# A lead-in whose last three tiles are mixed by way of HBM, and new lists that order it

## The chip, the cores and the metric

The kernel runs on one core of a Trainium2 chip. Its time is the device time of one launch in microseconds, the median of several runs. TensorE (PE) multiplies, VectorE (DVE) and ScalarE (ACT) work element by element, GpSimd (POOL) does little here, SyncE (SP) issues the DMA transfers, in the order of its program.

## What is computed

```python
# q, k, v: (8, 8, 576, 64); chunks of 64 rows, no work across chunks
scores = scale * q_c @ k_c^T                     # per chunk
attn   = exp(scores - max) / (sum + 1e-9)
x      = (attn @ v_c)  ->  (8, 576, 512)
# low-rank mix over the 576 rows of a batch, rank 32
u   = x + (x^T @ U @ V)^T
out = u + relu(u @ w_ch1) @ w_ch2                # 512 -> 2048 -> 512
```

All products of the mix and of the two layers are made from a high and a low part of each number (fp32r), three products for one.

## The kernel before

Eight batches are taken in four pairs of 2 × 576 rows, nine tiles of 128 rows each; a name such as u_6 or x_7 is a tile of the pair, and (1,2) is tile 2 of pair 1. Three tiles are a group. The weights are 16 chunks W0 to W15, each 512 KB, brought in raw and split into high and low parts (DVE lines 109 to 116 and 385). A block (g, f) takes group g through chunk f: twelve products of 384 columns make h (L815), ACT and DVE make hh and hl of it (L824, L829), and three sets of three products of 512 columns add to o (L842). Names are h_g_f; sc_1_0 are the scores (L541) and av_1_0 the weighted sums (L589) of tile 0 of pair 1.

The lead-in is everything up to the first block of group 2 of pair 0: the attention of the nine tiles of pair 0, the projection by U (y, ys), the mix (u, L748, then x + u on DVE, L754), the splitting of the weights and the 32 blocks of groups 0 and 1. A planner (order(), L161) writes its instructions out by hand. It takes the order of blocks on PE from STRETCHES, the order of SyncE's loads from LOADS (T5: q and k of tile 5; v5: its v, four transfers on L471; U, V, W0), and the rank of the other steps from WORK. HOLD delays two loads of v. The loads of v named in SOFT are issued from GpSimd's queue. After as many blocks as GATES names, the attention of tiles (1,0) and (1,1) may begin. From block HALVES_FROM on, one transfer a block copies a half of the heads of q or k of the next pair, rearranged, from HBM to HBM (halfq, halfk, L421, 2304 pieces of 128 B); the loads qn and kn (L453) of a tile of that pair read these copies, and DVE transposes them (qT, kT, L497).

For pairs 1 to 3, x + u goes out to HBM by four DMAs (us_td, L488, 2048 pieces of 128 B), comes back as one tile (us, L432), and is transposed by DVE (uT, L497). The exponentials of a tile go the same way (es_td, L493; es, L432; eT). In pair 0, u is transposed by four PE products for each tile (ut, L760). Then ACT casts (uth, L782) and DVE subtracts (utl, L787). For tiles 6 to 8 this happens after the last block of group 0.

After the lead-in a hand-written list sets the order of the main loop; its last string is LAST, for the last pair: one word for each o group of three products, u4 being the mix of tile 4, p4 the projection of tile 4, a dot nothing.

Of the kernel before, what the change touches and what calls it, by code (L numbers as in the profile page):

```python
# [23 lines left out]
def kernel(  # L24
# [23 lines left out]
    NF = DF // P  # L48
# [1 line left out]
    GT = 3  # L50
    NEARLY = 9
    PLAIN = 2
    SOFT = (2, 4)
    NX = 9
    SLOTS = {"qk": 3, "e": 1, "eT": 1, "vn": 2, "us": 1, "uT": 1}
    XROOM = 3
# [34 lines left out]
    w1 = {}  # L91
    w2 = {}
# [33 lines left out]
    rank = [0]  # L126
# [611 lines left out]
    def mix_ops(pr, t, x, ys, after=None, first=None):  # L738
        n = f"{pr}_{t}"
        st = {}  # L740
        g, j = divmod(t, GT)
# [49 lines left out]
        ad = Op("DVE", 0.69, add, lr, free="bank")  # L791
        if (pr, t) == (0, 0):
            Op("PE", 0.01, end_filling, lr, free="bank")
        if pr > 0:
            pu = Op("SP", 2.0, put_u, ad, lat=2.0)
            fe = Op("SP", 2.0, fetch_u, pu, take="us", lat=2.0)
            tr = Op("DVE", 0.71, square_u, fe, take="uT", free="us")
            hi = Op("ACT", 0.59, high, tr, take="" if j else "ut")
            lo = Op("DVE", 0.69, low, hi, free="uT")
            return [[lr, ad, pu], [fe], [tr, hi, lo]]  # L800
        tr = Op("PE", 0.55, transposed, ad, take="bank")
# [94 lines left out]

    LOADS = 'T0 v6 T1 v2 v7 U T2 T3 v1 T4 V v0 v3 W0 T5 T6 T7 T8 v5 W1 v8 W2 W3 W4 W5 W6 v4 W7 W8 W9 W10 W11 W12 W13 W14 W15'.split()
    WORK = 'W0 T8 T5 t6 t4 U W1 t8 w0 P0 T3 m5 t7 w1 T4 T2 t1 T6 m4 t3 W2 w2 W3 m2 W4 W5 t5 W6 W7 w3 V w4 m0 P1 W8 w5 w6 w7 t0 W9 W10 W11 T7 m3 w8 W12 w9 W13 w10 W14 T0 W15 T1 m1 w11 u0 w12 w13 w14 w15 t2'.split()  # L900
    STRETCHES = ((0, 0, 2), (1, 0, 1), (0, 2, 3), (1, 1, 3), (0, 3, 6), (1, 3, 5), (0, 6, 8), (1, 5, 7), (0, 8, 10), (1, 7, 8), (0, 10, 13), (1, 8, 14), (0, 13, 14), (1, 14, 16), (0, 14, 16))
    HOLD = {4: 3, 2: 1}
    GATES = (22, 27)
    TAIL = 6
    HALVES_FROM = 14
    BASE = 1000
    u_done = None
    v_done = []
# [1 line left out]
    xs = {}  # L910
    ys = {}
    his = {}
# [32 lines left out]
        lvs[t].after.append(tqs[h])  # L945
    prev = None
    blocks = 0
    halved = []
    second = halvings(2) + halvings(3)
    gates = dict(zip(GATES, range(len(GATES))))  # L950
    for g, f0, f1 in STRETCHES:
        for f in range(f0, f1):
            rank[0] = BASE
            prev = block_ops(0, g, f, f == 0, f == NF - 1, [*w_done[f], *mixed[g]], prev)
            blocks += 1
            if (g, f) == (0, NF - 1):
                last = prev
            if blocks >= HALVES_FROM and second:
                rank[0] = 0
                halved.append(Op("SP", 0.8, second.pop(0), prev[0], dma=2.75, n=2304, lat=2.0))  # L960
            if blocks in gates:
                rank[0] = 0
                assert len(halved) >= 8
                attention_ops(1, gates[blocks], prev[0], *halved[:8])
    assert blocks == 2 * NF
    rank[0] = 0
    for t in range(6, NT):
        m = mix_ops(0, t, last[0], ys, first=his.get(2))[1]
        his.setdefault(2, m[1])
    for o in ops:  # L970
        if o.eng != "PE" and o.rank[0] == BASE:
            o.rank = -1, o.rank[1]
        if o.name == "hidden":
            o.rank = BASE + 1, o.rank[1]
    rank[0] = BASE
    Op("SP", 3.8, lambda: load(1, len(GATES)), prev[0], take="qk qk vn")

# [298 lines left out]
    }  # L1276
    LAST = "t6 . q5 s6 . l3 n7 . f3 . t7 q6 . s7 u3 . n8 . p0 t8 . q7 s8 . p1 . p2 . q8 a8 . p3 p4 l4 l5 f4 l6 . u4 f5 l7 . u5 f6 l8 u6 f7 . u7 f8 u8"
    FIRST = "p0 p1 h t2 s2 n3 h . t3 . q2 s3 p2 n4 h h . t4 . q3 s4 p3 n5 h . t5 . q4 s5 h n6 p4 . l0 . f0 l1 . u0 f1 l2 . u1 f2 . . u2"

    def plan():  # L1280
# [95 lines left out]
```

## Time and profile before

| | us |
|---|---|
| median of three runs | 929.03 (927.85 to 929.34) |
| the profiled execution, its own time | 925.92 |
| span of that execution in the trace | 923.8 |
| PE busy, share of the span | 98% |
| DVE, ACT, POOL busy | 55%, 24%, 1% |
| DMA, busy share in the first tenth of the span | 0.9, 0.8, 0.9, 0.4 |

The page gives shares over the whole span. The lead-in takes the first 200 us, and there the shares differ: DVE is nearly full for 70 us of it. So the stages are read apart, in tables by window, and the passage from lead-in to main loop in order of time.

### The profile page before, as it was taken

Reading aid. Unit: us, or ns where it says so; the run is one execution under the profiler, and the core shown is the slowest. Engines: PE = TensorE matmul, PEld = TensorE weight load, DVE = VectorE, ACT = ScalarE, POOL = GpSimd, SP = SyncE. Lnnn points to the kernel's source line nnn. Section 1 sums busy time; section 2 is a strip of 40 time slices with the busy share of each in tenths; the row PEclk is TensorE's granted clock in tenths of the full one; section 3 lists DMA queues with packets and bytes.
Section 4 is the critical chain, followed back from the end, with each engine's and each line's share of the span. In section 5 each row is a group of like instructions: output and inputs, shape, how many; then the busy total and the mean of one; then the engine's idle time right before and its main releaser. Section 6 shows DMA issues by size and latency. Waiting matters only on the chain.

```text
span 923.8 us, 16154 instructions
## 1 busy us (share of the span) xinstructions
PE 907.5 (98%) x6594; PEld 797.0 (86%) x6594; DVE 511.3 (55%) x988; ACT 225.4 (24%) x399; POOL 9.7 (1%) x51
## 2 busy tenths in 40 slices
PE   8899999999999999999999999999999999999998
PEld 5569898888898888888898888998889888899886
DVE  4899994274546435544435635553443654678534
ACT  6545441121222111121211211111121121232211
POOL 2000000000000000000000000000000000000000
PEclk9999999999999999999999999999999999999999
DMA  9894477766537525644544624572241515000001
GB/s 185 190 332 138 138 155 110 119 162 147 127 73 179 117 52 138 130 118 91 126 78 105 137 64 109 129 145 71 69 92 34 149 47 113 37 1 1 0 1 69
DMA packets 278713, 98.79 MB, mean 107 GB/s; under 512 B 228464, under 2 KB 264944, under 8 KB 278640
## 3 DMA queue, kind: packets, MB, share of 16 engines
q1 hardware_dynamic: 278384, 97.24, 45.8%
q8 instruction: 52, 0.85, 0.4%
q0 software_dynamic: 256, 0.52, 0.3%
q14 instruction: 21, 0.17, 0.1%
HBM read 73.84 MB, written 37.75 MB: 121 GB/s over the span
## 4 chain that ended last, share of the span: by engine, by line
PE 85%; DVE 6%; DMA 4%; SPq 3%; ACT 2%; issue 1%; ACTq 0%; DVEq 0%
PE o L842 39%; PE h L815 34%; PE p L1162 5%; PE av L589 2%; PE sc L541 2%; DMA wraw<-in_moe_w_ch_dram 2%; SPq L471 1%; PE ps_fill L154 1%; PE y L704 1%; PE y L705 1%; PE u L748 1%; DMA us<-us_3d 1%; DVE w L385 1%; DVE wroom L113 1%; DVE hl L829 1%
## 5 line engine op out<-in xcount | busy, mean ns | idle before, releaser
L815 PE MATMUL h<-uth,w 128*128 128x384 f32 x1344 | 365.0, 337 | 0.8 <-DVE hl L829 0.5
L842 PE MATMUL o<-w,hh 128*128 128x512 f32 x1152 | 347.5, 394 | 0.0
L815 PEld LDWEIGHTS h<-uth,w 128*128 128x128 f32 x1344 | 245.2, 188 | 8.6 <-issue 1.5
L842 PEld LDWEIGHTS o<-w,hh 128*128 128x128 f32 x1152 | 213.7, 188 | 37.4 <-issue 0.5
L815 PE MATMUL h<-utl,w 128*128 128x384 f32 x672 | 226.2, 337 | 0.3 <-DVE utl L787 0.2
L842 PE MATMUL o<-w,hl 128*128 128x512 f32 x576 | 214.1, 395 | 1.0 <-DVE hl L829 1.0
L824 ACT ACTIVATE hh<-h 128x384 fp32r<-128x384 f32 x168 | 82.3, 490 | 367.1 <-PE h L815 366.9
L829 DVE SCALAR_TENSOR_TENSOR hl<-h,hh 128x384 fp32r<-128x384 f32 x168 | 91.9, 548 | 125.5 <-ACT hh L824 125.4
L815 PEld LDWEIGHTS h<-utl,w 128*128 128x128 f32 x672 | 126.1, 188 | 6.4 <-DVE utl L787 1.0
L842 PEld LDWEIGHTS o<-w,hl 128*128 128x128 f32 x576 | 107.5, 188 | 25.3 <-DVE hl L829 1.8
L497 DVE STREAM_TRANSPOSE uT<-us 128x512 f32<-128x512 f32 x27 | 29.6, 1097 | 43.9 <-PE h L815 19.4
L497 DVE STREAM_TRANSPOSE eT<-es 128x512 f32<-128x512 f32 x27 | 29.2, 1081 | 41.3 <-DMA es<-es_7d 8.9
L497 DVE STREAM_TRANSPOSE qT<-qn 128x512 f32<-128x512 f32 x27 | 19.2, 709 | 53.4 <-PE h L815 50.3
L570 ACT ACTIVATE ex<-ex 128x512 f32<-128x512 f32 x36 | 22.8, 634 | 65.4 <-DVE ex L562 61.0
L555 DVE TENSOR_REDUCE mx<-sc 128x4 f32<-128x256 f32 x72 | 28.0, 414 | 14.7 <-PE sc L541 14.7
L693 ACT CAST xh<-x 128x512 fp32r<-128x512 f32 x30 | 18.6, 619 | 66.7 <-DVE x L608 45.4
L754 DVE TENSOR_TENSOR x<-u,x 128x512 f32<-128x512 f32 x36 | 24.4, 686 | 16.8 <-PE u L748 16.6
L782 ACT CAST uth<-uT 128x512 fp32r<-128x512 f32 x27 | 16.5, 620 | 50.3 <-DVE uT L497 50.3
L608 DVE TENSOR_TENSOR x<-av,sm 128x256 f32<-128x256 f32 x72 | 27.2, 417 | 0.9
L697 DVE TENSOR_TENSOR xl<-x,xh 128x512 fp32r<-128x512 f32 x30 | 20.6, 686 | 8.8 <-ACT xh L693 8.0
L589 PEld LDWEIGHTS av<-vn,eT 64*64 64x64 f32 x864 | 15.6, 133 | 10.4 <-issue 10.4
L854 DVE TENSOR_TENSOR x<-o,x 128x512 f32<-128x512 f32 x36 | 23.3, 678 | 1.7 <-PE o L842 1.7
(127 smaller groups left out, 672.0 us busy)
## 6 DMA issues: line engine op xcount, KB each, us to landing
wraw<-in_moe_w_ch_dram SPq DMA_DIRECT2D x32, 512.0 KB
out_dram<-x SPq DMA_DIRECT2D x36, 256.0 KB
halfq<-in_q_dram SPq DMA_DIRECT2D x24, 288.0 KB
halfk<-in_k_dram SPq DMA_DIRECT2D x24, 288.0 KB
qn<-halfq SPq DMA_DIRECT2D x27, 256.0 KB
kn<-halfk SPq DMA_DIRECT2D x27, 256.0 KB
vn<-in_v_dram SPq DMA_DIRECT2D x108, 64.0 KB
qkv<-in_q_dram SPq DMA_DIRECT2D x8, 256.0 KB
```

The source lines that it names most:

```text
L497: turned = nc.vector.transpose(dst, src)
L555: nc.vector.reduce_max(mx, st["sc"][e], axis=AX.X)
L570: nc.scalar.activation(exf, exf, AF.Exp, scale=SCALE)
L589: nc.tensor.matmul(ps[e][cs, hp * D1 : (hp + 1) * D1], lhsT=st["eT_"][rows, hp, cs], rhs=vn[rows, c, hp, :], start=True, stop=True,)
L608: nc.vector.tensor_mul(by_head[:, heads(pr, t, e), :], st["av"][e][:, :, 0:D], st["sm"][:, e].unsqueeze(2).broadcast_to([P, HP, D]),)
L754: nc.vector.tensor_add(x, st["u"], x)
L815: o = nc.tensor.matmul(ps[:, :GN], lhsT=w[:, z, cc], rhs=u[:, cc, :], start=(n == 0), stop=(n == 3 * NCC - 1))
L824: nc.scalar.activation(hh, ps[:, :GN], AF.Relu)
L829: nc.vector.scalar_tensor_tensor(hl, ps[:, :GN], 0.0, hh, op0=ALU.max, op1=ALU.subtract)
L842: nc.tensor.matmul(acc[g, j], lhsT=h[:, js], rhs=w2[f][:, z], start=(first and i == 0), stop=(final and i == 2),)
L854: nc.vector.tensor_add(x, ps, x)
L1162: nc.tensor.matmul(ps[:, :GN], lhsT=w[x][c], rhs=u[y][c], start=(n == 1), stop=(n == 3 * CC))
```

## The change

The loads of v for tiles 2 and 4 go to SyncE's queue (SOFT empty). The mix of tiles 6 to 8 of pair 0 takes the way over HBM that the later pairs take, and each tile is mixed after a block of group 0 of its own: tile 6 after h_0_9, tile 8 after h_0_13, tile 7 after h_0_15. Its puts and fetches have a rank ahead of other transfers. A step on PE that issues no instruction stands at the end of the lead-in and waits for these tiles. LOADS, WORK, STRETCHES, HOLD, GATES and HALVES_FROM are new; group 0 now ends before group 1. In LAST a dot moves.

```diff
-    SOFT = (2, 4)
+    SOFT = ()
...
-        if pr > 0:
-            pu = Op("SP", 2.0, put_u, ad, lat=2.0)
-            fe = Op("SP", 2.0, fetch_u, pu, take="us", lat=2.0)
-            tr = Op("DVE", 0.71, square_u, fe, take="uT", free="us")
-            hi = Op("ACT", 0.59, high, tr, take="" if j else "ut")
+        if pr > 0 or g == 2:
+            pu = Op("SP", 2.6, put_u, ad, dma=2.5, n=2048, lat=2.0)
+            fe = Op("SP", 0.6, fetch_u, pu, take="us", dma=1.3, n=512, lat=2.0)
+            pu.rank = fe.rank = -2, t
+            tr = Op("DVE", 1.1, square_u, fe, take="uT", free="us")
+            hi = Op("ACT", 0.59, high, tr, first, take="" if j else "ut")
...
-    HOLD = {4: 3, 2: 1}
-    GATES = (22, 27)
+    HOLD = {}
+    MIXED_AFTER = {6: 9, 7: 15, 8: 13}
+    GATES = (22, 23)
     TAIL = 6
-    HALVES_FROM = 14
+    HALVES_FROM = 15
...
-            if (g, f) == (0, NF - 1):
-                last = prev
+            if g == 0:
+                first_blocks.append(prev[0])
...
+    u_last = []
     for t in range(6, NT):
-        m = mix_ops(0, t, last[0], ys, first=his.get(2))[1]
+        m = mix_ops(0, t, xs[t], ys, first_blocks[MIXED_AFTER[t]], first=his.get(2))[-1]
         his.setdefault(2, m[1])
+        u_last.append(m[2])
...
+    rank[0] = BASE + 2
+    Op("PE", 0.01, lambda: None, *u_last)
...
-    LAST = "t6 . q5 s6 . l3 n7 . f3 . t7 q6 . s7 u3 . n8 . p0 t8 . q7 s8 . p1 . p2 . q8 a8 . p3 p4 l4 l5 f4 l6 . u4 f5 l7 . u5 f6 l8 u6 f7 . u7 f8 u8"
+    LAST = "t6 . q5 s6 . l3 n7 . f3 . t7 q6 . s7 u3 . n8 . p0 t8 . q7 s8 . p1 . p2 . q8 a8 . p3 p4 . l4 l5 f4 l6 u4 f5 l7 . u5 f6 l8 u6 f7 . u7 f8 u8"
```

SyncE at the passage into the main loop, before (out_dram is the store of a finished tile, es_1 the fetch of exponentials, qn_2 and kn_2 are q and k of tile (1,2)):

```order
L493 DMA es_1d<-ex_1_2028 128x4x128
L432 DMA es_1_2063<-es_1d 128x512
L860 DMA out_dram<-x_4_549 128x512
L860 DMA out_dram<-x_5_883 128x512
L453 DMA qn_2_2113<-halfq_1439 128x2x256
L453 DMA kn_2_2114<-halfk_1608 128x2x256
L471 DMA vn_2_2115<-in_v_dram 64x4x64 x4
```

and after, from the fetch of us_7 on:

```order
L432 DMA us_7_2103<-us_7d 128x512
L493 DMA es_1d<-ex_1_2038 128x4x128
L432 DMA es_1_2130<-es_1d 128x512
L421 DMA halfk_1662<-in_k_dram 9x256x32 x3
L421 DMA halfq_2252<-in_q_dram 9x256x32
L861 DMA out_dram<-x_3_522 128x512
L861 DMA out_dram<-x_4_577 128x512
L471 DMA vn_3_2314<-in_v_dram 64x4x64
L861 DMA out_dram<-x_5_883 128x512
L453 DMA qn_2_2211<-halfq_1500 128x2x256
L453 DMA kn_2_2212<-halfk_1662 128x2x256
```

Four halves and a part of vn_3 stand between es_1 and qn_2, where none stood.

PE at the same place, before (ut are the transposes that the change takes out, vst the low-rank factor):

```order
L748 MATMUL u_6_2109<-ys_1_994,vst 128x512
L748 MATMUL u_7_2123<-ys_1_994,vst 128x512
L748 MATMUL u_8_2126<-ys_1_994,vst 128x512
L842 MATMUL o_0_950<-w_1628,hh_0_14_2085 128x512 x2
L842 MATMUL o_0_950<-w_1628,hl_0_14_2087 128x512
L760 MATMUL ut_6_2133<-ident,x_6_834 128x128 x4
L842 MATMUL o_1_954<-w_1628,hh_0_14_2085 128x512 x2
L842 MATMUL o_1_954<-w_1628,hl_0_14_2087 128x512
L760 MATMUL ut_7_2146<-ident,x_7_964 128x128 x4
L760 MATMUL ut_8_2153<-ident,x_8_970 128x128 x4
L589 MATMUL av_1_1_2160<-vn_1_1931,eT_1_2151 64x65 x2
```

and after:

```order
L843 MATMUL o_3_1081<-w_1691,hh_1_15_2156 128x512 x2
L843 MATMUL o_3_1081<-w_1691,hl_1_15_2159 128x512
L843 MATMUL o_4_1087<-w_1691,hh_1_15_2156 128x512 x2
L843 MATMUL o_4_1087<-w_1691,hl_1_15_2159 128x512
L843 MATMUL o_5_1095<-w_1691,hh_1_15_2156 128x512 x2
L843 MATMUL o_5_1095<-w_1691,hl_1_15_2159 128x512
L589 MATMUL av_1_1_2182<-vn_1_1900,eT_1_2172 64x65 x2
```

The three u stand earlier, in the blocks behind h_0_9, h_0_13 and h_0_15, the transposes are gone, and av_1_1 stands behind the last o. Behind it come, before and after, two h of group 2 and then the scores of (1,2).

SyncE at the head, before:

```order
L318 DMA vraw<-in_moe_V_dram 128x288
L471 DMA qkv_0_93<-in_v_dram 64x4x64 x4
L471 DMA qkv_3_137<-in_v_dram 64x4x64 x4
L359 DMA wraw_407<-in_moe_w_ch_dram 128x4x256
L363 DMA wraw_407<-in_moe_w_ch_dram 128x1024
L459 DMA qkv_5_442<-in_q_dram 128x8x64
L459 DMA qkv_5_442<-in_k_dram 128x8x64
L328 DMA vall<-vroom 32x4x144 x4
```

and after:

```order
L471 DMA qkv_2_155<-in_v_dram 64x4x64 x4
L318 DMA vraw<-in_moe_V_dram 128x288
L359 DMA wraw_378<-in_moe_w_ch_dram 128x4x256
L363 DMA wraw_378<-in_moe_w_ch_dram 128x1024
L471 DMA qkv_4_268<-in_v_dram 64x4x64 x4
L459 DMA qkv_5_460<-in_q_dram 128x8x64
L459 DMA qkv_5_460<-in_k_dram 128x8x64
L328 DMA vall<-vroom 32x4x144 x4
```

The v of tiles 2 and 4 (qkv_2, qkv_4) stand now in this queue, that of tile 4 behind W0.

## Rows read from the trace of the kernel before

**Rows 1.** The page: engines with busy us, share of the span, instructions.

```profile
PE 907.5 (98%) x6594; PEld 797.0 (86%) x6594; DVE 511.3 (55%) x988; ACT 225.4 (24%) x399; POOL 9.7 (1%) x51
```

**Rows 2.** Stages: start:end, length, busy us by engine, granted clock, DMA share, GB/s.

```profile
0.00:60.00 60.00, 52.37 (x777) 35.25 (x778) 43.24 (x117) 33.40 (x59) 6.77 (x25) 1.00 0.94 218
60.00:130.00 70.00, 68.70 (x349) 61.75 (x349) 68.86 (x87) 33.78 (x46) 0.00 (x0) 1.00 0.55 167
130.00:181.00 51.00, 51.00 (x286) 46.12 (x285) 21.61 (x39) 10.46 (x20) 0.11 (x1) 1.00 0.74 125
181.00:205.00 24.00, 22.75 (x202) 19.09 (x200) 17.93 (x37) 5.56 (x11) 0.22 (x2) 1.00 0.66 150
```

**Rows 3.** PE in order of time: start, length, instruction, count [idle before, releaser].

```profile
151.17 0.34 PE L815 MATMUL h<-uth,w 128*128 128x384 f32 x1
...
182.64 0.50 PE L842 MATMUL o<-w,hl 128*128 128x512 f32 x1 [0.78 <-DVE hl L829]
...
192.25 0.86 PE L748 MATMUL u<-ys,vst 128*128 128x512 f32 x3
192.95 0.63 PE L842 MATMUL o<-w,hh 128*128 128x512 f32 x2
...
195.07 1.13 PE L760 MATMUL ut<-ident,x 128*128 128x128 f32 x8
196.60 0.70 PE L589 MATMUL av<-vn,eT 64*64 64x65 f32 x32 [0.40 <-issue]
...
205.29 0.69 PE L541 MATMUL sc<-kT,qT 64*64 64x64 f32 x32
```

**Rows 4.** SyncE's issues in order of time, at the passage.

```profile
191.27 0.33 SPq L432 DMA_DIRECT2D es<-es_1d  x1
191.69 0.86 SPq L860 DMA_DIRECT2D out_dram<-x  x2
192.60 0.49 SPq L453 DMA_DIRECT2D qn<-halfq  x1
193.19 0.56 SPq L453 DMA_DIRECT2D kn<-halfk  x1
```

**Rows 5.** DVE in order of time, the transpose of es_1.

```profile
195.40 1.10 DVE L497 STREAM_TRANSPOSE eT<-es 128x512 f32<-128x512 f32 x1
```

**Rows 6.** Size of a half (page); two windows of halves; GB/s, 110:215 in 40 slices.

```profile
halfq<-in_q_dram SPq DMA_DIRECT2D x24, 288.0 KB
...
160.00:161.00 1.00, 1.00 (x7) 0.92 (x6) 0.00 (x0) 0.63 (x1) 0.00 (x0) 1.00 0.92 98
180.00:181.00 1.00, 1.00 (x7) 1.00 (x7) 0.05 (x1) 0.00 (x0) 0.00 (x0) 1.00 0.78 122
...
GB/s 33 362 115 20 336 152 98 227 259 100 83 108 96 5 119 98 259 97 106 147 47 155 102 59 109 246 99 107 74 133 73 161 343 138 117 161 240 175 198 203
```

**Rows 7.** SyncE, the way of u over HBM in the main loop.

```profile
254.03 2.05 SPq L488 DMA_DIRECT2D us_0d<-x  x4
...
257.60 0.33 SPq L432 DMA_DIRECT2D us<-us_0d  x1
```

**Rows 8.** The head of the lead-in: SyncE, then DVE, then PE.

```profile
19.57 3.29 SPq L471 DMA_DIRECT2D qkv<-in_v_dram  x5
...
24.76 0.37 SPq L459 DMA_DIRECT2D qkv<-in_q_dram  x1
...
25.93 5.45 SPq L328 DMA_DIRECT2D vall<-vroom  x4
...
52.02 0.69 DVE L109 TENSOR_SCALAR wroom<-wroom 128x1024 f32<-128x1024 f32 x1 [1.05 <-ACT wroom L98]
...
66.78 0.33 PE L815 MATMUL h<-uth,w 128*128 128x384 f32 x1
```

**Rows 9.** PE at the very start, the filling products.

```profile
1.56 4.88 PE L154 MATMUL ps_fill<-fill 128*128 128x512 bf16 x11 [1.56 <-DVE fill L147]
```

**Rows 10.** PE in the last pair, u_4's second product and u_5's.

```profile
765.82 0.73 PE L748 MATMUL u<-ys,vst 128*128 128x512 f32 x2 [0.69 <-DVE ys L730]
```

More of the change, by code (lines that the diff above doesn't have):

```diff
@@ L893 @@
     Op.name = ""
-    LOADS = 'T0 v6 T1 v2 v7 U T2 T3 v1 T4 V v0 v3 W0 T5 T6 T7 T8 v5 W1 v8 W2 W3 W4 W5 W6 v4 W7 W8 W9 W10 W11 W12 W13 W14 W15'.split()
-    WORK = 'W0 T8 T5 t6 t4 U W1 t8 w0 P0 T3 m5 t7 w1 T4 T2 t1 T6 m4 t3 W2 w2 W3 m2 W4 W5 t5 W6 W7 w3 V w4 m0 P1 W8 w5 w6 w7 t0 W9 W10 W11 T7 m3 w8 W12 w9 W13 w10 W14 T0 W15 T1 m1 w11 u0 w12 w13 w14 w15 t2'.split()
-    STRETCHES = ((0, 0, 2), (1, 0, 1), (0, 2, 3), (1, 1, 3), (0, 3, 6), (1, 3, 5), (0, 6, 8), (1, 5, 7), (0, 8, 10), (1, 7, 8), (0, 10, 13), (1, 8, 14), (0, 13, 14), (1, 14, 16), (0, 14, 16))
-    HOLD = {4: 3, 2: 1}
-    GATES = (22, 27)
+    LOADS = 'T0 v3 v1 T1 U T2 v0 T3 T4 v2 V W0 v4 T5 T6 T7 T8 v6 v5 W1 v8 v7 W2 W3 W4 W5 W6 W7 W8 W9 W10 W11 W12 W13 W14 W15'.split()
+    WORK = 't4 m0 W0 T7 m5 T3 t3 W1 T8 t8 T5 w0 w1 m3 T4 m4 w2 t7 W2 P0 t6 t1 W3 W4 w3 T2 W5 w4 T1 T6 t0 w5 m2 W6 w6 w7 W7 U w8 w9 T0 u0 w10 W8 m1 V W9 w11 t5 W10 W11 w12 W12 W13 P1 W14 t2 w13 w14 w15 W15'.split()
+    STRETCHES = ((0, 0, 2), (1, 0, 2), (0, 2, 4), (1, 2, 3), (0, 4, 5), (1, 3, 7), (0, 5, 8), (1, 7, 8), (0, 8, 11), (1, 8, 9), (0, 11, 12), (1, 9, 10), (0, 12, 15), (1, 10, 12), (0, 15, 16), (1, 12, 16))
+    HOLD = {}
+    MIXED_AFTER = {6: 9, 7: 15, 8: 13}
+    GATES = (22, 23)
     TAIL = 6
-    HALVES_FROM = 14
+    HALVES_FROM = 15
     BASE = 1000
@@ L947 @@
     blocks = 0
+    first_blocks = []
     halved = []
```

## The prediction

> **What bounds the kernel now.** I read the row of the engines on the page first: TensorE is busy for 907.5 of the 923.8 us [rows 1]. So a change matters only where it adds or removes TensorE's work or idle time. Next comes the table by stages [rows 2]. TensorE stands idle for 7.6 us of the first 60, for 1.3 us of the next 70 (where VectorE, with 68.86 of 70, has no time left either), never from 130 to 181, and for 1.25 us between 181 and 205, where the lead-in passes into the main loop. All that the change moves lies in these stages, but for one product in the last pair. Then I read the passage itself in order of time [rows 3], SyncE's queue beside it [rows 4], and the rate at which the transfers run [rows 6]. The reader should see in rows 4 that SyncE issues in program order, and that behind the fetch of es_1 (191.27) come only two outs, qn and then kn (193.19): this kn is k of tile (1,2), whose scores start at 205.29 without a wait [rows 3].
>
> **The empty step and the string LAST.** The step issues no instruction. In LAST one dot moves: u_4's first product goes from behind the first of three o groups to behind the second. The wait of 0.69 us [rows 10] is that of u_4's second product for ys_1, and the same instructions stand ahead of it afterwards: 0.
>
> **u of tiles 6 to 8.** Out go twelve TensorE transposes: the last eight take 1.13 us and 0.40 us of idle time follows [rows 3]; twelve are 1.7 us. With them the wait of 0.78 us for hl at 182.64 may go, since the blocks stand in another order. That makes up to 1.7 + 0.4 + 0.8 = 2.9 us on TensorE at the passage. In come, for each tile, four put DMAs (four issues took 2.05 us, and the fetch was issued 3.6 us after the first [rows 7]), one fetch, and one transpose on VectorE. VectorE has free time from 130 on (21.61 of 51 us busy [rows 2]), so the transposes cost nothing. The casts and subtractions are as before.
>
> **The transfers.** This is the term that decides. Prices: a half is 288 KB in pieces of 128 B; with only halves running, the rows show 98 to 122 GB/s [rows 6], so 2.4 to 3.0 us; I take 2.75. A tile's put has 2048 such pieces, 256 KB: 2.1 to 2.7 at the same rates; I take 2.3. Whole rows run at 336 to 362 GB/s in the best slices [rows 6], so a q, k, e or u tile of 256 KB takes 0.8 us at least; the vn tile and the put of es, in pieces between the two, I put at 2.1 and 1.4, as estimates between these ends. An out is 0.75.
>
> First what the row shows: short pieces move at a third of the rate of whole rows [rows 6]. The Trainium skill ("DMA: Bandwidth & Descriptors", Specifications) says that full rate wants at least 512 B in a transfer and that below it the engine reads, modifies and writes. The rows agree in direction, and the rule speaks against this change, which adds 3 × 2048 pieces of 128 B; it gives no price, so the sum goes by the rows.
>
> Now the queue after the change. The 23rd block's h begins at 151.2 [rows 3], about 151.6 afterwards, and the half that waits for it starts to move near 155. From there the order of SyncE's instructions has no gap: half 2.75, qn_0 0.8, us_8's puts 2.3, kn_0 0.8, vn_0 2.1, half 2.75, us_8 0.8, qn_1 0.8, kn_1 0.8, vn_1 2.1, es_0's put 1.4 = 17.4, to 172.4. The fetch of es_0 waits for that put, and goes out near 174.5; then the fetch 0.8, two halves 5.5, us_7's puts 2.3, three outs 2.25, a half 2.75, us_7 0.8, es_1's put 1.4 = 15.8, to 190.3. So es_1 goes out near 191.7, much as before (191.27 [rows 4]), and av_1_1, whose transpose came 4.1 us after the fetch [rows 4, 5], is in time to within a microsecond. Behind es_1 stand now what stood earlier before: three halves 8.25, a half of the next pair 2.75, three outs and a part of vn 2.75, qn_2 0.8, kn_2 0.8 = 15.35, ahead of them the fetch's own 0.8. With 192.5 for es_1's landing kn_2 is there at 207.9, its transpose (0.7) at 208.7, and the scores of (1,2) can start at 208.9. They stand behind two h in TensorE's order, and TensorE, 2.9 us early, gets there near 202.4: it stands for some 6.5 us. Against 205.29 before, that is **+3.6 us**: the gain at the passage is inside this sum and is lost in the wait. Bounds: with the halves and puts at 2.4 and 2.1 us, the three runs of transfers come out 1.0, 1.3 and 1.4 us shorter, so 3.6 - 3.7, about 0; at 3.0 and 2.7 they are 0.9, 1.2 and 1.0 longer, +6.7, and then av_1_1 waits too, within the same sum.
>
> **Waits added on VectorE.** qT_1 stands ahead of hl_1_11 and waits for qn_1, and uT_8 and uT_7 stand ahead of other hl. If these are late, TensorE's o wait, as they did for 0.78 us at 182.64 [rows 3] behind kT. Taken at 0.6 us; like the gain it is covered by the wait for the scores, and it would cost 0.6 to 1.5 us without it.
>
> **The head of the queue.** The loads of v for tiles 2 and 4 leave GpSimd's own queue for SyncE's, where issues of this kind follow each other without a pause: five in 3.29 us, 0.65 each [rows 8]. Eight more are 5.2 us, all ahead of tile 5's q and k, which went out at 24.76. Given back: four vall DMAs held SyncE for 5.45 us [rows 8], 2.85 more than four issues of 0.65; a SyncE that comes to them later meets less of that wait; and the v of tiles 6 and 7 moves behind tile 8's loads, where nobody waits for it yet. That leaves 5.2 - 2.85 = 2.35, rounded down to 2 for the last point. It is not lost elsewhere: the v of tile 4 stands now behind W0, so x of tile 4, y and the first mix come later by these issues, and VectorE's first step on W1 (52.02, after 1.05 us of idle time [rows 8]) by about as much; from 60 on VectorE is full [rows 2], so that what starts late there stays late. I put that step at 54 and the first h of group 1 at 69 instead of 66.78 [rows 8]: **+2 us**, which shifts all that follows, the gates of the halves too. Bounds: -1 (a wait of this stage, such as the 1.05, falls away with the order) to +4 (5.2 less 1.4, if SyncE meets half of vall's wait again).
>
> The Trainium skill ("Trainium Kernel Development and Optimization", Key Constraints) says that DMAs of SP, ACT and POOL run on the same 16 engines and that issuing from several saves only issue time. Issue time is what is short here, so this too speaks against the change; by it alone the cost would be the 5.2 us of issues.
>
> **TensorE's clock after the stand.** In the trace the first eleven filling products of 512 columns take 4.88 us, 0.44 each, after an engine that had done nothing; later three products of 512 columns begin at 192.25 and the next work at 192.95, 0.23 each [rows 3, 9]. So 0.44 is the pace of the 1.2 GHz level and 0.23 that of 2.4, although the column of the granted clock reads 1.00 for the whole stage [rows 2]. The start costs 11 × 0.21 = 2.3 us. After 0.69 us of idle time two products take 0.73 with their tail [rows 10]: nothing lost. A stand of 6.5 us is nearer to the start than to this one: **+2.1** (ten products slow), bounds 0 and 2.3. The Trainium skill ("TensorE: Matmul & The Clock Gate", What's actually happening) says that an array that has idled runs at 1.2 GHz until it has been busy for a while. By this page the loss is certain and not only likely; no run here shows it after a stand in the middle.
>
> **Sum:** 3.6 + 2 + 2.1 + 0 = **+7.7 us**. The profiled execution takes 925.92 us (span 923.8 and 2.1 around it), 3.1 less than the median of the runs, 929.03. The same 7.7 on the median gives 936.7.
>
> **Rivals.**
> (a) *The queue is empty in time (faster).* If short pieces move at the rate of the best row, 122 GB/s, throughout, and whole rows hide between them, kn_2 lands before TensorE comes to the scores; it has to come 6.5 us sooner, over some 53 us of queue. The fast bound gives 3.7 of these, and the other 2.8 must come from transfers that overlap. From there the wait is gone, no clock is lost, and the 2.9 us at the passage stay. With the head between -1 and +1 that is -2 to -4: 926.1. Against it: only one of the rows is at that rate, and kn_2 stands behind fifteen microseconds of transfers that cannot be issued ahead of es_1.
> (b) *The two cancel (within 0.2%).* The queue at its fast bound (0 at the scores), the head at +1, no clock lost: about 930.
> (c) *No clock lost.* The stand comes in two parts (av_1_1 first), so TensorE has work between: 3.6 + 2 = 934.6. A slower case of its own.
> (d) *The queue at its slow bound.* 6.7 + 4 + 2.3 = 13.0, 942.0.
> (e) *The change doesn't do what it says:* the fetches of us wait in SyncE so long that the mix isn't ready before h of group 2. For it: SyncE stands at each fetch until its puts have landed, 3.6 us from the first issue [rows 7]. Against: us_7, the last, lands some 7 us ahead of its use. It would add one or two us to (d).
>
> **Chances.** The forecast's own path 0.45, (c) 0.15, (d) with (e) 0.10: slower 0.70. (a) 0.17: faster. (b) 0.13: same. 0.2% is 1.9 us, about what a measurement of this kernel can tell from no change. The range reaches from (a), 926, to above (d), 943.
>
> **What would show it.** In the profile after: a wait of some 6.5 us of "sc" for kT or kn near 202 to 210, with kn's third issue near 205 instead of 193.19; h of group 2 starting a little earlier or level (the head's 2 us against the 2.9); the first h of group 1 near 69; products after the stand at 0.44 us for a while; the wait of u for ys near 765 still at 0.7; twelve transposes of ut fewer. The forecast is wrong if kn's issue stays below 197, if h of group 1 starts before 67, or if a wait inside the lead-in's blocks (an hl behind uT or qT) exceeds 2 us.

## The result, and the profile after

The changed kernel takes 941.22 us (median of four runs, 940.61 to 941.63); the kernel before takes 928.44 beside it. The ratio is 1.0137, with a 95% interval from 1.0119 to 1.0154: 12.8 us slower. The profiled execution takes 941.07 us, with a span of 939.1, against 923.8 before. That is 15.3 us more; 2.5 of them come from the profiled execution of before, which was that much under its own median.

The page of the changed kernel: the engines as in [rows 1], then the busy tenths of PE and the granted clock in 40 slices.

```profile
PE 910.6 (97%) x6580; PEld 798.3 (85%) x6585; DVE 513.7 (55%) x991; ACT 225.8 (24%) x399; POOL 4.8 (1%) x43
...
PE   8889999987999999999999999999999999999998
...
PEclk9999999998999999999999999999999999999999
```

PE dips in slices 9 and 10, from 188 to 235 us, and the granted clock in slice 10; nowhere else behind the lead-in's head and ahead of the end. The table by stages, as in [rows 2] with the stage behind them:

```profile
0.00:60.00 60.00, 49.84 (x732) 33.34 (x740) 39.93 (x108) 32.08 (x58) 1.82 (x17) 0.97 0.82 186
60.00:130.00 70.00, 68.82 (x369) 60.12 (x370) 68.17 (x87) 34.01 (x44) 0.00 (x0) 1.00 0.54 183
130.00:181.00 51.00, 49.62 (x279) 44.38 (x278) 27.41 (x51) 12.16 (x23) 0.11 (x1) 1.00 0.73 136
181.00:205.00 24.00, 24.00 (x205) 20.89 (x204) 15.63 (x33) 4.35 (x8) 0.22 (x2) 1.00 0.81 141
205.00:300.00 95.00, 86.05 (x681) 76.27 (x680) 45.03 (x95) 17.22 (x32) 0.45 (x4) 0.96 0.60 133
```

From 181 to 205 TensorE has no idle time left, and the 1.25 us of before are gone. In the stage behind it, it stands idle for 9 us. Where, the order of time shows (PE; the last product ahead of the stand, the scores of (1,2) with the idle time ahead of them, and the products after it):

```profile
203.06 0.44 PE L816 MATMUL h<-uth,w 128*128 128x384 f32 x1
...
208.07 0.40 PE L705 MATMUL y<-xl,ust 128*128 128x512 f32 x1
217.16 1.13 PE L541 MATMUL sc<-kT,qT 64*64 64x64 f32 x32 [8.69 <-DVE kT L497]
218.22 1.22 PE L843 MATMUL o<-w,hh 128*128 128x512 f32 x2
...
219.66 1.05 PE L843 MATMUL o<-w,hh 128*128 128x512 f32 x2
...
221.49 0.34 PE L816 MATMUL h<-uth,w 128*128 128x384 f32 x1
```

DVE stood as long, for qn_2, and then transposed q and k:

```profile
215.59 0.71 DVE L497 STREAM_TRANSPOSE qT<-qn 128x512 f32<-128x512 f32 x1 [8.40 <-DMA qn<-halfq]
216.39 0.71 DVE L497 STREAM_TRANSPOSE kT<-kn 128x512 f32<-128x512 f32 x1
```

SyncE, from the fetch of es_1 to kn_2, to be read against [rows 4]:

```profile
196.18 0.32 SPq L432 DMA_DIRECT2D es<-es_1d  x1
196.54 6.97 SPq L421 DMA_DIRECT2D halfk<-in_k_dram  x3
203.61 3.00 SPq L421 DMA_DIRECT2D halfq<-in_q_dram  x1
206.72 3.56 SPq L861 DMA_DIRECT2D out_dram<-x  x2
210.41 0.65 SPq L471 DMA_DIRECT2D vn<-in_v_dram  x1
211.16 0.55 SPq L861 DMA_DIRECT2D out_dram<-x  x1
212.08 0.38 SPq L453 DMA_DIRECT2D qn<-halfq  x1
212.51 0.48 SPq L453 DMA_DIRECT2D kn<-halfk  x1
```

Before, 1.9 us lay between the fetch of es_1 and kn_2 [rows 4]; now 16.3 us do. SyncE's rows follow each other there without a gap: the first of the four halves is issued in 0.76 us, the other three in some 3 each, and so is the first store.

I compared the same product of both kernels in time, block by block. The first h of group 1 is 4.3 us late (71.09 against 66.78 [rows 8]), the 25th block's h 4.4; the first h of group 2 is 3.0 late (203.06 against 200.10), the scores 11.9 (217.16 against 205.29 [rows 3]), the third h of group 2 13.4 (221.49 against 208.10). Some 1.2 us are added until 300, in steps of 0.2 to 0.5, and 0.8 later. The place of the loss is thus plain: the head with 4.3 us; then the stand (the idle time ahead of the scores) with 8.7 and 1.5 of slow clock behind it; against them stand the 2.7 us that the passage saved, less a wait of 1.25.

### The profile page after: what moved, and what is told of

It is laid out like the page before. It is cut to its first block, busy times and chain, and to the rows that moved or that the text cites. A ratio compares the mean times of both kernels' runs of the same rounds, so it can differ in the third digit from the quotient of the medians.

```text
span 939.1 us, 16132 instructions
## 1 busy us (share of the span) xinstructions
PE 910.6 (97%) x6580; PEld 798.3 (85%) x6585; DVE 513.7 (55%) x991; ACT 225.8 (24%) x399; POOL 4.8 (1%) x43
## 4 chain that ended last, share of the span: by engine, by line
PE 78%; DVE 10%; SPq 5%; DMA 4%; issue 1%; ACT 1%; DVEq 0%; ACTq 0%
PE o L843 36%; PE h L816 31%; PE p L1169 5%; SPq L471 3%; PE av L589 2%; DVE wroom L116 2%; PE sc L541 1%; DVE wroom L113 1%; DVE w L385 1%; DMA us<-us_3d 1%; DMA wraw<-in_moe_w_ch_dram 1%; DVE hl L830 1%; PE u L748 1%; SPq L459 1%; DMA us_3d<-x 1%
## 5 line engine op out<-in xcount | busy, mean ns | idle before, releaser
L497 DVE STREAM_TRANSPOSE uT<-us 128x512 f32<-128x512 f32 x30 | 33.0, 1100 | 47.7 <-PE h L816 21.1
L555 DVE TENSOR_REDUCE mx<-sc 128x4 f32<-128x256 f32 x72 | 27.8, 411 | 13.4 <-PE sc L541 13.4
L754 DVE TENSOR_TENSOR x<-u,x 128x512 f32<-128x512 f32 x36 | 24.4, 686 | 17.2 <-PE u L748 17.1
L782 ACT CAST uth<-uT 128x512 fp32r<-128x512 f32 x30 | 18.4, 620 | 57.8 <-DVE uT L497 56.3
L541 PE MATMUL sc<-kT,qT 64*64 64x64 f32 x864 | 18.5, 223 | 8.9 <-DVE kT L497 8.7
L787 DVE TENSOR_TENSOR utl<-uT,uth 128x512 fp32r<-128x512 f32 x30 | 20.5, 687 | 9.6 <-ACT uth L782 9.6
L541 PEld LDWEIGHTS sc<-kT,qT 64*64 64x64 f32 x864 | 15.8, 138 | 11.2 <-DVE kT L497 9.8
```

The source lines that it names most:

```text
L497: turned = nc.vector.transpose(dst, src)
L541: nc.tensor.matmul(ps[e][cs, hp * C : (hp + 1) * C], lhsT=st["qT_"][rows, hp, cs], rhs=st["kT_"][rows, hp, cs], start=True, stop=True,)
L555: nc.vector.reduce_max(mx, st["sc"][e], axis=AX.X)
L754: nc.vector.tensor_add(x, st["u"], x)
```

## The experiments

All are timed beside the kernel before, whose medians in the four sessions were 929.6, 928.7, 928.8 and 928.5; the ratios are to the kernel before in the same session, and the changed kernel's own is 1.0137.

### The loads of (1,2) first

```diff
-    Op("SP", 3.8, lambda: load(1, len(GATES)), prev[0], take="qk qk vn")
+    ahead = Op("SP", 3.8, lambda: load(1, len(GATES)), prev[0], take="qk qk vn")
...
-    for o in order():
+    plan_of = order()
+    plan_of.remove(ahead)
+    plan_of.insert(plan_of.index(halved[13]), ahead)
+    for o in plan_of:
```

> The changed kernel with one thing moved: the loads qn_2, kn_2 and vn_2 of tile (1,2) stand in SyncE's order right behind the fetch of es_1, ahead of the three halves of k, the half of the next pair and the outs. Theory (the order of SyncE is the cause of the stand of 8.7 us ahead of the scores of (1,2)): kn_2 is issued near 197 instead of 212.5, the stand is gone and so is the slow clock after it (1.45 us), and the time falls by about 10 us, from 941.2 to about 931. Rival (the queue as a whole is too full from 155 on): the delay moves on to es_1's users, to the halves and to tiles (1,3) and (1,4), other waits of together 4 us or more appear, and the time falls by 6 us at most.

Measured: 941.14 us, ratio 1.0116 (1.0093 to 1.0138): nothing gained that the intervals could tell. The stand moved. SyncE, DVE and PE of this run:

```profile
198.67 1.02 SPq L453 DMA_DIRECT2D kn<-halfk  x1
...
202.48 6.88 SPq L421 DMA_DIRECT2D halfk<-in_k_dram  x3
...
220.54 2.38 SPq L453 DMA_DIRECT2D qn<-halfq  x1
```

```profile
225.55 0.71 DVE L497 STREAM_TRANSPOSE qT<-qn 128x512 f32<-128x512 f32 x1 [13.38 <-DMA qn<-halfq]
226.18 0.52 DVE L830 SCALAR_TENSOR_TENSOR hl<-h,hh 128x384 fp32r<-128x384 f32 x1
```

```profile
226.76 1.22 PE L843 MATMUL o<-w,hl 128*128 128x512 f32 x2 [6.62 <-DVE hl L830]
```

kn_2 goes out at 198.67 and the scores of (1,2) wait for nothing. But now q of the next tile, (1,3), is issued at 220.54, behind the same halves; its transpose stands on VectorE ahead of an hl, and TensorE waits 6.62 us for that hl. The third h of group 2 comes 8.7 us sooner than in the changed kernel, the fifth 0.8 us later. My theory that the order of the loads is the cause falls in this form; the rival, that the queue is behind as a whole, holds. The clock falls with this wait too: it is 0.50 from 225 to 230.

### The loads of v planned onto GpSimd again, alone and with the loads of (1,2) first

```diff
-    SOFT = ()
+    SOFT = (2, 4)
...
-    HOLD = {}
+    HOLD = {4: 3, 2: 1}
```

> The changed kernel with v of tiles 2 and 4 loaded from GpSimd's queue again, with the two holds of the kernel before; everything else, the lists too, as changed. Theory (SyncE's issue time is what the head pays): the first h of group 1 comes 4 us sooner, at 67 instead of 71.1, and the time falls by 3 to 4 us, to 937 to 938; the stand ahead of the scores stays at 8 to 9 us since the gates of the queue move with the blocks. Rival (the new lists are the cause, above all the late W1 and x of tile 8): the first h of group 1 stays within 1 us of 71, and the time within 1.5 us.

> Both of the edits before together: the loads of (1,2) behind the fetch of es_1, and v of tiles 2 and 4 from GpSimd's queue. If the two causes are independent the gains add: about 10 and 3 to 4 us, 927 to 928, and the 2.9 us saved at the passage show for the first time, so level with the kernel before (928.4) or 1 us below it. If they share a cause (the queue comes free sooner when the head is shorter), the sum is smaller than the parts by 2 us or more.

Measured: 955.52 (1.0273, 1.0253 to 1.0294) and 965.39 (1.0386, 1.0361 to 1.0411). Both expectations missed. With SOFT set back, the planner works out the head anew from lists that were made for the other case; in the first of the two the fourth block's h comes 13 us later than in the changed kernel. So neither run says anything on SyncE's issue time. They do say that these LOADS and WORK don't fit the old setting of SOFT, and that the question needs an edit that leaves the orders alone. That is what the runs with v from the other queue do, below.

### The kernel before, with its last four halves ahead of qn_2

```diff
-    Op("SP", 3.8, lambda: load(1, len(GATES)), prev[0], take="qk qk vn")
+    behind = Op("SP", 3.8, lambda: load(1, len(GATES)), prev[0], take="qk qk vn")
...
-    for o in order():
+    plan_of = order()
+    for h in halved[12:]:
+        plan_of.remove(h)
+    at = plan_of.index(behind)
+    plan_of[at:at] = halved[12:]
+    for o in plan_of:
```

> The kernel before with the last four halves of k moved in SyncE's order to stand right ahead of qn_2 (they stood 12 to 28 us sooner); nothing else. Theory: four halves of 2.75 us put kn_2's landing from about 196 to about 207, its transpose to 208, the scores of (1,2) from 205.3 to about 208.5: a stand of 3 us, and the time rises by 3 us, to 931.5, and to 933 if the clock falls after a stand of this length too. Rival (transfers behind es_1 overlap enough, and the stand in the changed kernel has another cause): within 1 us of 928.4.

Measured: 941.95 (1.0129, 1.0104 to 1.0154), as slow as the changed kernel, without any other part of the change. SyncE and PE:

```profile
193.60 10.35 SPq L421 DMA_DIRECT2D halfk<-in_k_dram  x4
203.99 3.02 SPq L453 DMA_DIRECT2D qn<-halfq  x1
207.06 0.46 SPq L453 DMA_DIRECT2D kn<-halfk  x1
```

```profile
211.59 1.14 PE L541 MATMUL sc<-kT,qT 64*64 64x64 f32 x32 [5.28 <-DVE kT L497]
```

The direction is right, the size was too small by 8 to 9 us: 12.4 measured on the medians, 3 expected and 4.5 with the clock. The stand is 5.28 us where I had said 3; the clock falls with it (0.50 from 211 to 216); and a wait of 1.03 for hl and one of 1.37 ahead of the weighted sums of (1,2) follow, for what was late behind the halves. From the block ahead of the scores to six blocks behind it the profile falls back by 11.6 us: the eleven microseconds of transfers, put at this place, are paid in full.

### Three halves handed on to the main loop

The loads of (1,2) stand first here too, by the edit shown above; these lines are added.

```diff
+    handed = [o.run for o in halved[13:]]
+    for o in halved[13:]:
+        plan_of.remove(o)
...
-    to_halve = [w for b in range(4, B) for w in halvings(b)]
+    to_halve = handed + [w for b in range(4, B) for w in halvings(b)]
...
-    FIRST = "p0 p1 h t2 s2 n3 h . t3 . q2 s3 p2 n4 h h . t4 . q3 s4 p3 n5 h . t5 ...
+    FIRST = "p0 p1 . t2 s2 n3 h h t3 h q2 s3 p2 n4 h h h t4 h q3 s4 p3 n5 h . t5 ...
```

> The changed kernel with 8 us of transfers taken out of the passage: the last three halves of k of pair 1 (needed only by tile (1,4)) go to the main loop, in the places where it copies its first halves of pair 2, which slide back by three; and the loads of (1,2) stand behind the fetch of es_1, as in the run with kn first. Theory now (a backlog in SyncE's queue: whatever stands behind the last halves is late by their length, kn_2 in the changed kernel, qn_3 in the run with kn first): both stands are gone or under 2 us together, the clock stays up, and the time falls from 941.2 by about 10 us to 931. Rival (the halves cost the same wherever they stand before tile (1,4)): a stand of 5 us or more appears at kn_4 or es_2, and the time stays above 937.

Measured: 940.5 (1.0117, 1.0093 to 1.0142). The h behind the scores comes 9.9 us sooner than in the changed kernel, counted from the block ahead of them, and all of that is lost again within five blocks. Tile (1,2)'s weighted sums wait 3.93 us, until the transpose of es_2 has ended, and those of (1,3) wait 2.94 us for that of es_3; behind each of the two waits the granted clock is at 0.50 for two to three microseconds. SyncE, DVE and PE:

```profile
216.98 0.41 SPq L493 DMA_DIRECT2D es_2d<-ex  x1
```

```profile
222.94 1.08 DVE L497 STREAM_TRANSPOSE eT<-es 128x512 f32<-128x512 f32 x1 [2.71 <-DMA es<-es_2d]
```

```profile
224.12 0.75 PE L589 MATMUL av<-vn,eT 64*64 64x65 f32 x30 [3.93 <-issue]
```

The put of es_2 stands in SyncE behind kn_3, and kn_3 behind the handed halves. The time is the rival's again, though its one stand of 5 us came in two parts: ahead of tile (1,4) these halves cost the same at the two places tried.

### v of tiles 2 and 4 from the other queue, with all orders kept

In the changed kernel from GpSimd, and in the kernel before from SyncE; the planner doesn't know of it, so that nothing else moves.

```diff
 # in the changed kernel
-                queue = nc.gpsimd if plain(pr, t) and t in SOFT else nc.sync
+                queue = nc.gpsimd if plain(pr, t) and t in (2, 4) else nc.sync
 # in the kernel before
-                queue = nc.gpsimd if plain(pr, t) and t in SOFT else nc.sync
+                queue = nc.sync
```

> The changed kernel with every engine's order as it is, but the eight transfers of v of tiles 2 and 4 issued by GpSimd in place of SyncE. Unlike the run with the loads planned anew, the order of SyncE, VectorE and TensorE is the same. Theory (SyncE's issue time costs the head its 4.3 us): the first h of group 1 starts 3 us or more sooner, at 68 or below instead of 71.1, and the time falls by about 3 to 938. Rival (the lists, which put both late W1 and the first mixes late, cost it): within 1 us of 71.1, and the time within 1.5 us of 941.

> The kernel before with every engine's order as it is, but the eight transfers of v of tiles 2 and 4 issued by SyncE, where GpSimd issued them. The other half of the same question. Theory (issue time of SyncE): the first h of group 1 comes 2.4 us later (eight issues of 0.65 less what vall waits less), 69 instead of 66.8, and the time rises by 2 to 3 us to 931 or 932. Rival (SyncE has slack there): within 1 us of 66.8 and of 929.

Measured: 943.0 (1.0141, 1.0114 to 1.0168) and 934.05 (1.0053, 1.0032 to 1.0074). In the kernel before, the eight issues cost 5.4 us, twice what I had expected: the first h of group 1 comes at 73.6 in its profile. (The ratio, 1.0053, makes it 4.9.) In the changed kernel giving them back is worth nothing. Its first h of group 1 starts at 68.52, 2.6 us sooner than in the profile of the changed kernel, but the stand ahead of the scores is 1.1 us longer (9.8), and runs with the changed kernel's own head came out there too: 68.13, 68.58, 68.97, 69.7 and 72.0 in other experiments. The head varies by some 4 us from one profile to another, and one profile can't settle a term of 2 us. The five other heads and that of the changed kernel have a mean of 69.8; three profiles with the head of the kernel before (66.78, and two experiments, 68.08 and 69.33) have 68.1. By these profiles the new lists have made room for most of what the move costs, and the head is left 1.7 us late on average. A part of the spread is TensorE's clock: of the six profiles with the changed kernel's head the two latest (71.09 and 72.03) are the two in which the granted clock falls to 0.50 between 56 and 62; in the other four it is 1.00 from 44 to 80.

### The way over HBM, in the kernel before

The whole g == 2 case of mix_ops as the change has it, and MIXED_AFTER = {6: 9, 7: 12, 8: 13} are put into the kernel before; the rest is as it was.

```diff
-        if pr > 0:
+        if pr > 0 or g == 2:
...
+    MIXED_AFTER = {6: 9, 7: 12, 8: 13}
...
-        m = mix_ops(0, t, last[0], ys, first=his.get(2))[1]
+        m = mix_ops(0, t, xs[t], ys, first_blocks[MIXED_AFTER[t]], first=his.get(2))[-1]
```

> The kernel before with one part of the change alone: tiles 6, 7 and 8 are mixed behind h_0_9, h_0_12 and h_0_13 and go by HBM and VectorE; lists, SyncE's loads and LAST as before. It takes twelve transposes from TensorE and adds about 9 us of transfers. Theory (the route itself is worth its 2.9 us at the passage, and the backlog comes from the lists that put the halves late): group 2's h starts 2 to 3 us sooner than at 200.1, the scores of (1,2) wait less than 3 us, and the time lies between 926 and 930. Rival (the 9 us of transfers alone make the backlog): a stand of 5 us or more ahead of the scores of (1,2) or of (1,3), and 934 or more.

Measured: 937.29 (1.008, 1.0054 to 1.0106), 8.6 us slower than before (7.4 by the ratio). The theory falls, and the time is the rival's; but the stand is another than the rival named, 4.17 us ahead of the weighted sums of (1,1) and none at the scores. Between the 16th block and group 2 TensorE comes 4.3 us behind: waits of 2.4 us for x and 0.4 for hl among the blocks and the 4.17, less what the route gives back, near 3 by this balance. Behind the stand the granted clock is 0.50 from 206 to 209, and another 1.6 us are lost by the third h of group 2. For the stand the profile names v, but that load was issued at 184; what ended just then is the transpose of es_1, whose fetch went out at 200.72 in place of 191.27 [rows 4]. SyncE, DVE, PE:

```profile
200.72 0.34 SPq L432 DMA_DIRECT2D es<-es_1d  x1
```

```profile
204.51 1.07 DVE L497 STREAM_TRANSPOSE eT<-es 128x512 f32<-128x512 f32 x1
```

```profile
205.84 1.14 PE L589 MATMUL av<-vn,eT 64*64 64x65 f32 x32 [4.17 <-DMA vn<-in_v_dram]
```

### The halves from the 12th block, alone and with v from GpSimd

```diff
-    HALVES_FROM = 15
+    HALVES_FROM = 12
```

> The changed kernel with one number changed: the halves of pair 1 may begin after the 12th block instead of the 15th. TensorE's and VectorE's orders stay as they are; SyncE's first half goes out some 12 us sooner, into time in which the queue has room, and no half stands behind es_1 any more. Theory now (from 155 to 235 the DMA queue is the bound, because it got 9 us of puts and fetches and starts its halves at 124.5 instead of 111.9): the backlog shrinks by up to 12 us, the stand of 8.7 us ahead of the scores and the slow clock behind it go, no stand of more than 2 us takes their place, and the time falls from 941 to about 931. Rival (the queue is full before 155 too, by the weights): the weights come late instead, with waits of TensorE between 80 and 150, or a stand of 5 us or more stays; the time is above 936.

> The halves from the 12th block, and the eight transfers of v of tiles 2 and 4 issued by GpSimd with every other order kept, as in the run with v from GpSimd. There the head gained 2.6 us and the stand grew by as much, since the queue set the end. If the halves from the 12th block take the queue off the path, the head's gain shows now: 2 to 3 us below the run with the halves alone, near 928 to 929, level with the kernel before or a little under it. If the queue still bounds, the two runs are within 1 us of each other.

Measured: 937.42 (1.0084, 1.0054 to 1.0114) and 939.23 (1.0105, 1.007 to 1.0139). The scores of (1,2) no longer wait. But my sentence that TensorE's order stays was false: with the halves elsewhere the planner set the other engines' steps anew too, and in the two traces some 240 of TensorE's 6580 products and some 50 of VectorE's 991 instructions stand in another order, the first at 125. Between 130 and 205 the longest waits of the first run are these:

```profile
PE h L816 <- DVE hl L830: 4.3, 2, 2.5
PE h L816 <- DVE x L754: 1.5, 1, 1.5
PE o L843 <- DVE hl L830: 1.1, 1, 1.1
```

With a slow clock from 165 to 170 (0.66 on average) behind one of them the first h of group 2 is 3.9 us later than in the changed kernel, where the 16th block had been 2.9 us earlier. The run shows that the stand can be taken away by an earlier start of the halves, not what that alone is worth. The second run differs from the first by nothing that the intervals tell apart: once more the loads of v bring nothing in these lists.

### The changed kernel without the way over HBM

```diff
-        if pr > 0 or g == 2:
+        if pr > 0:
...
-    MIXED_AFTER = {6: 9, 7: 15, 8: 13}
+    MIXED_AFTER = {6: 15, 7: 15, 8: 15}
```

> The changed kernel without the way of u over HBM: tiles 6 to 8 are mixed by TensorE's transposes, all three behind h_0_15 (they find no PSUM banks sooner). Lists, SyncE's loads and LAST as changed, halves from the 15th block. The queue loses 9 us of puts and fetches, and one half stands between es_1 and qn_2 instead of four. Theory (backlog): the stand ahead of the scores of (1,2) falls from 8.7 to 2 us or less, the passage loses 2 to 3 us to the transposes, the head keeps its 4 us: 933 to 935. Rival (the late start of the halves alone makes the backlog): a stand of 5 us or more here or at (1,3), 938 or more.

Measured: 932.05 (1.0041, 1.0023 to 1.0059), 9.2 us under the changed kernel's 941.22 and 1 us better than expected. LOADS, WORK, STRETCHES, GATES and LAST are those of the change; the planner's order from 130 on follows from them anew. SyncE and PE there:

```profile
193.29 0.76 SPq L421 DMA_DIRECT2D halfk<-in_k_dram  x1
194.10 2.92 SPq L453 DMA_DIRECT2D qn<-halfq  x1
197.08 0.45 SPq L453 DMA_DIRECT2D kn<-halfk  x1
```

```profile
206.68 0.45 PE L541 MATMUL sc<-kT,qT 64*64 64x64 f32 x12
```

One half stands where four stood, and the scores wait for nothing. Taken together with the run that added the way over HBM to the kernel before (+8.6 us), this shows which part of the change costs most of the time: the lists without the way over HBM are 3.3 us slower than before (932.05 against 928.75 in that session), with it 12.8. What the 3.3 consist of beyond the head's 1.7 wasn't separated.

### The same bytes in larger pieces

```diff
-        moved = nc.sync.dma_start(
-            halves[pr, z][odd * n : (odd + 1) * n, 2 * e + g].rearrange("n s (h i) -> n s h i", i=SQ),
-            (q, k)[z][b, e * HP : (e + 1) * HP, :, g * SQ : (g + 1) * SQ].rearrange("h (n s) i -> n s h i", s=C),
-        )
+        to = halves[pr, z][odd * n : (odd + 1) * n, 2 * e + g].rearrange("n s (h i) -> n s h i", i=SQ)
+        of = (q, k)[z][b, e * HP : (e + 1) * HP, :, g * SQ : (g + 1) * SQ].rearrange("h (n s) i -> n s h i", s=C)
+        if pr == 1:
+            h0 = 2 * (2 * e + g)
+            to = halves[pr, z][odd * n : (odd + 1) * n, 2 * e + g].rearrange("n (x y) p -> x n (y p)", y=4)
+            of = (q, k)[z][b, h0 : h0 + 2].rearrange("h s i -> (h s i)").rearrange("(n x c) -> x n c", n=n, x=16)
+        moved = nc.sync.dma_start(to, of)
```

> The changed kernel with the order of every engine and the bytes of every transfer as they are; but the sixteen halves of pair 1 are moved in 144 pieces of 2 KB instead of 2304 of 128 B. The rearrangement that the small pieces are for is left out, so q and k of pair 1 arrive in the wrong places; all engines do the same work on them. A half should take about 0.9 us instead of 2.75 to 3, the rate of the other transfers in whole rows. Theory (the stand is the time of short pieces in one queue, and nothing in the order of TensorE, VectorE or SyncE needs it): the 30 us shorter queue lets kn_2 land before it is wanted, the stand of 8.7 us and the 1.5 us of slow clock are gone, no other stand over 2 us takes their place, the time falls by 9 to 11 us to 930 to 932. Rival (the waits in SyncE's order, for puts to land, for exponentials and for blocks, make the stand): kn_2 is still issued after 206, a stand of 4 us or more stays, 936 or more. In the run with the halves from the 12th block TensorE's order had changed as well (the planner set the blocks' products in another order), so that one could not tell.

Measured: 934.16 (1.0066, 1.0048 to 1.0085), 7 us under the changed kernel, at the same order of TensorE, VectorE, ScalarE and SyncE throughout. It lies between the theory and the rival. From 130 to 181 the DMA engines are busy for 0.47 of the time in place of 0.73, and SyncE issues a half in 0.6 to 0.9 us in place of up to 3.1. The stand falls to 3.1 us: most of it was the time of short pieces, and a part was not. SyncE, DVE (the last step on x_3) and PE:

```profile
196.16 0.88 SPq L427 DMA_DIRECT2D halfq<-in_q_dram  x1
200.22 1.52 SPq L864 DMA_DIRECT2D out_dram<-x  x2
...
203.99 0.49 SPq L456 DMA_DIRECT2D kn<-halfk  x1
```

```profile
199.51 0.68 DVE L858 TENSOR_TENSOR x<-o,x 128x512 f32<-128x512 f32 x1
```

```profile
209.33 0.69 PE L544 MATMUL sc<-kT,qT 64*64 64x64 f32 x32 [3.09 <-DVE kT L500]
```

SyncE has nothing to do from 197.0 to 200.2. It waits at the store of x_3, which VectorE finished at 200.2, after the last block of group 1; the loads of (1,2) are behind it in program order. Of the 8.7 us, 5.6 went with the short pieces; the 3.1 that stay I put down to a second cause, the stores of the group that now ends last, which stand ahead of qn_2. That is argued from the order, since moving the stores alone was not tried. In the changed kernel the second cause would be covered by the first, since SyncE comes to the stores at 206.7 only.

## Why the prediction was right, and where its sizes were off

Forecast were +7.7 us, 936.7 on the median, in a range from 926 to 943; measured are +12.8 and 941.2, near the upper end. A range that wide would have held most outcomes. What bears the forecast out is the rows: the stand is at the product that it named, kn_2's issue has moved to 212.51 (it had said near 205), and the clock falls behind the stand.

**The queue at the passage: the mechanism held, the size was 6 us short.** It said that kn_2 would be late behind three halves of k, a half of the next pair and three stores, that the scores of (1,2) would wait for it, and that the passage's gain would vanish inside this wait. The trace shows each step. The stand was put at 6.5 us and is 8.69; the scores were put at +3.6 and the head's 2, +5.6 in all, and are at +11.9. Of the missing 6.3 us, 2.3 are the head of this profile, and the rest is in the queue. es_1 goes out at 196.18, 2.5 us later than the sum's 191.7 with the head's 2; that is about the same 2.3. The run of transfers behind it was put at 17.2 us, from es_1's issue to the scores, and took 21.0 (196.18 to 217.16). Two things were left out there. The sum took a load as usable the moment its transfer ends, and the transpose as next: the row of qT begins 3.5 us after qn_2's issue. And the four halves took some 12 us in place of 11, by the rate in these windows:

```profile
198.00:210.00 12.00, 10.47 (x81) 8.85 (x79) 7.79 (x15) 3.23 (x6) 0.11 (x1) 1.00 0.80 106
199.00:204.00 5.00, 5.00 (x53) 4.03 (x52) 4.70 (x8) 1.24 (x2) 0.11 (x1) 1.00 0.87 104
```

At 104 GB/s a half of 288 KB takes 2.84 us, close to the 2.75 of the sum; the rest are gaps between them. In the 12 us 1.27 MB moved, and the four halves are 1.18 of these.

**What the sum didn't see at all** is that qn_2 could not have gone out before 204 in this profile in any case, in the order that SyncE has. VectorE finished x_5 at 204.2:

```profile
202.93 1.27 DVE L855 TENSOR_TENSOR x<-o,x 128x512 f32<-128x512 f32 x2
```

The stores ahead of it belong to the group that ends last, and before the change that was the other group. The sum counted these stores' 2.25 us of transfer and not what they wait for.

**u of tiles 6 to 8.** The gain at the passage was put at up to 2.9 us. Measured: the lateness falls from 4.4 at the 25th block to 3.0 at group 2, by 1.4, with a wait of 1.25 for hl ahead of u_7 in between. So the saving itself is about 2.7. That wait was put at 0.6 with 1.5 as its upper end; like the gain it is covered by the stand.

**The head:** put at +2 with bounds -1 and +4. The profile after has +4.3, with a stretch at 0.50 of the clock in it; the mean over six profiles is +1.7. The working behind it (0.65 us for an issue) gave 2.4 for an order left as it was; the kernel before with v in SyncE lost 5.4, about twice that, and the new lists win a part back. That the head came out near the sum is luck: two errors cancelled.

**The clock after the stand:** put at 2.1, and 1.5 us measured, from the scores (+11.9) to the third h of group 2 (+13.4). The windows behind the stand show the level:

```profile
217.00:220.00 3.00, 2.84 (x36) 2.43 (x37) 1.96 (x6) 0.22 (x1) 0.00 (x0) 0.50 0.59 139
220.00:222.00 2.00, 2.00 (x9) 1.63 (x8) 0.00 (x0) 0.41 (x1) 0.00 (x0) 0.85 0.44 115
```

0.50 is the 1.2 GHz level. It agrees with the Trainium skill ("TensorE: Matmul & The Clock Gate", What's actually happening), by which an idle array is throttled until activity releases it. The loss is smaller than at the start, where the slow products took 4.88 us [rows 9]; here the products are at full pace again from 220.8.

**LAST and the empty step** were put at 0. The wait of u for ys is 0.7 in both kernels, and the lateness is 15.2 us on either side of the place. The empty step has no row.

**Rivals.** (a), the queue empty in time, was out of reach in this order: even with the halves in large pieces 3.1 us of stand remain. (b) and (c) fell with the stand, which came in one piece and with the slow clock. (d), the queue at its slow bound with a head of 4, comes nearest: it named 13.0 us, and 12.8 were measured on the median. (e) didn't come: utl of the last of the three tiles was ready at 200.9, ahead of the first h of group 2 at 203.06. Some 2 us that the profile loses between 230 and its end have no experiment; the profiles of the kernel before with late halves and of the changed kernel without HBM lose 1.4 and 1.7 there against the same profile, so that a part may lie in that one, which was 2.5 us under its median.

The Trainium skill's warning ("DMA: Bandwidth & Descriptors", Specifications) that transfers under 512 B run below full rate spoke against this change, and the run with pieces of 2 KB bears it out: 5.6 us less stand with the same bytes.

## What to carry to other kernels

A detour that takes 2 us of work off the busiest engine isn't free because the engine it goes to has time: its transfers take their place in a queue, and whatever stands behind them in program order pays. Before giving a queue more work, add up what it has to move between two fixed points in time, and look for loads behind stores that can't leave yet; moving one load ahead only hands the wait to the next one as long as the sum doesn't fit. And an experiment that lets a planner work anew changes more than its edit says: force the order, or compare the orders before reading the time.

## What the runs showed of the hardware that was not expected

The granted clock can fall when TensorE has already resumed: in the run with larger pieces, after the stand of 3.1 us, it is 1.00 until 210, 0.92 in the next microsecond and 0.50 from 211 on. The products right behind the stand ran at full speed (0.73 us for two), later ones at half (1.06 for two, from 211.9):

```profile
210.00:211.00 1.00, 1.00 (x8) 0.87 (x5) 0.94 (x3) 0.00 (x0) 0.00 (x0) 0.92 0.51 111
211.00:212.00 1.00, 1.00 (x4) 0.72 (x3) 0.47 (x2) 0.49 (x1) 0.00 (x0) 0.50 0.81 233
```

Behind the 0.69 us of idle time in [rows 10] the products had kept their full pace. In the run with the halves handed on, the wait of 3.93 us ended at 224.1, and the clock fell at 225. In the head of the changed kernel an idle time of 1.78 us, with 0.45 and 0.17 shortly behind it, was followed by a granted clock of 0.50 from 57 to 60.

An issue on SyncE can last as long as a transfer. In the changed kernel the first half behind es_1 was issued in 0.76 us, the next two and that of the next pair in 2.97, 3.08 and 3.00, and the store of x_3 behind them in 3.09, though VectorE had finished x_3 at 202.4; at 104 GB/s a half takes 2.84. With the halves in pieces of 2 KB the same issues last 0.34 to 0.88.

With one and the same order in the head, the first h of group 1 starts between 68.1 and 72.0 from profile to profile, while the medians of the kernel before agree within 1.2 us from session to session.
